# Block-causal attention before two feed-forward layers: split fp32r operands against unsplit fp32 on parts of the TensorE array

## The chip, the cores and the metric

The kernel runs on one core of a Trainium2 chip. The metric is the device time of one execution in microseconds (us). TensorE (PE) multiplies, VectorE (DVE), ScalarE (ACT) and GpSimd (POOL) do the rest, and one queue (SP) issues every DMA. The working memory is SBUF; TensorE writes to PSUM, which has eight banks of 512 fp32 columns on 128 partitions.

## The reference

```python
def _attn_ref(q, k, v):                 # 4 batches, 8 heads, 576 positions, 64 channels
    scores = np.matmul(q, k.transpose(0, 1, 3, 2)) / np.sqrt(64)
    mask = pos[:, None] // 64 >= pos[None, :] // 64      # causal by blocks of 64
    scores = np.where(mask, scores, -1e9)
    attn = np.exp(scores - scores.max(-1, keepdims=True))
    attn = attn / (attn.sum(-1, keepdims=True) + 1e-09)
    return np.matmul(attn, v)

x = attn_out with its heads side by side                  # 2304 tokens x 512
h = x @ w_in;  x = (h * sigmoid(h)) @ w_out               # 512 -> 2048 -> 512
h = x @ w2_in; x = (h * sigmoid(1.702 * h)) @ w2_out
```

## The kernel before

The 32 heads are worked in 16 pairs: head A of a pair lies on partitions 0 to 63, head B on 64 to 127. Queries and keys come with the channels on partitions, 576 positions in the free direction, in nine bands (`j`) of 64 queries. Band `j` needs keys 0 to 64 (j + 1), so its scores have 64 to 576 columns.

TensorE multiplies in fp32r, a form of which one pass over the array keeps only part of the fp32 digits. So every operand is split into a high half (a copy rounded to fp32r) and a low half (the rest), and each product is three: high by high, high by low, low by high. For the scores (`s_mm`, lines 452 to 454) the queries of both heads are laid out block-diagonally in a tile `bd`, so that one 128 x 128 weight tile makes a band of 64 queries of both heads. `q_hi`, `q_lo`, `k_hi` and `k_lo` make the halves, `q_put` lays the query halves into `bd` by DMA. `s_max` takes the row maxima from PSUM on VectorE, `s_exp` the exponential and the row sums on ScalarE. `t_mm` (line 517) transposes the probabilities by TensorE, four 128 x 128 blocks to a bank, 25 blocks a pair. `t_hi` copies a bank out as the high half, `t_lo` (line 535) subtracts for the low half. `o_mm` (line 554) multiplies by the values, whose halves `v_hi` and `v_lo` make: the weights are high and low values side by side, 64 columns each, and the high and low probabilities stream past them. So the result has the part of the high values on the upper 64 partitions and that of the low values on the lower ones, for each head, in two ranges of bands (`halves`). `o_copy` takes these out of PSUM, `x_shift` moves three halves by DMA between partitions, `x_add` adds them on GpSimd and `x_norm` (line 587) multiplies by the reciprocals of the row sums. The reciprocals go through `r_add`, `r_inv`, a transpose (`r_mm`), `r_copy`, a write to DRAM (`r_put`) and a read that spreads them over 64 partitions (`r_get`).

The result `xy` has 512 channels on four groups of 128 partitions and 2304 tokens. The feed-forward layers (`phase`, `evac`) take up to 512 tokens at a time: per 128 hidden channels 12 products up (lines 697 to 699), tanh, and 12 down (lines 724 to 726). The weights come as fp64 and are turned into fp32 and split on VectorE, ScalarE and GpSimd (`w_scale` to `w_split`, lines 265 to 306), two pieces per 128 hidden channels.

The order of instructions is worked out at build time. Each piece of work is an `Op` with an engine, an expected duration, what it reads and writes, and an urgency. `Flow.run` goes through expected time and always gives an engine its most urgent piece that is ready. For attention the urgency is in `plan`, one number for each step of a pair, and `TAU` from pair to pair; attention goes ahead of the feed-forward layers (`BEFORE`). `EARLY` holds back single weight pieces. The engines then work in that order, each waiting for what it needs. At the start `NWARM` products on zeros run until the first scores.

SBUF is shared in time. Attention's tiles lie in pools `a1` to `a6`; a pool that attention has finished with is closed, and a pool of the feed-forward layers (`l1` to `l6`) opens in its place. `HOME` says which pool a feed-forward tile lies in, so the first weight tiles wait for the first pools of attention to close.

Of the kernel before, what the change touches and what calls it, by code (L numbers as in the profile page):

```python
# [22 lines left out]
class Op:  # L23
    __slots__ = ("eng", "us", "fn", "at", "lag", "size", "left", "outs", "ready", "end", "name", "idx", "sb")


class Flow:
# [3 lines left out]
    SEM = 0.06  # L31
    LAG = {"pe": 0.2, "act": 0.1, "dve": 0.08, "pool": 0.04, "sp": 0.0, "none": 0.0}
# [6 lines left out]
    def add(self, eng, us, fn, reads=(), writes=(), at=0.0, lag=0.0, size=0, after=(), name="", sb=False, early=0.0):  # L39
        op = Op()  # L40
        op.eng, op.us, op.fn, op.at, op.lag, op.size, op.name = eng, us, fn, at, lag, size, name
        op.outs, op.ready, op.end, op.idx, op.sb = [], early, 0.0, len(self.ops), sb
# [35 lines left out]
    def run(self, log=None):  # L78
# [3 lines left out]
        dma = 0.0  # L82
        now = {}
# [7 lines left out]
        while n < len(self.ops):  # L91
# [11 lines left out]
            us = op.us  # L103
            other = "pool" if op.sb else "dve" if e == "pool" and self.dve_sb else None
# [24 lines left out]
def act(n):  # L129
    return 0.06 + n * 0.833e-3  # L130
# [14 lines left out]
def block_causal_attention_two_ffn(  # L145
# [25 lines left out]
    NS = 10  # L171
    NWF = 8
    EARLY = [40.4, 125.4, 119.6, 162.9, 164.5, 84.4, 75.8, 216.7, 81.4, 12.3, 74.1, 229.3]
# [3 lines left out]
    NWARM = 12  # L177
    TAU = 12.6
# [11 lines left out]
    stacks = {x: ExitStack() for x in ("a1", "a2", "a3", "a4", "a5", "a6")}  # L190
    pools = {"cst": open_pool(ctx, "cst"), "psum": open_pool(ctx, "psum", space=PSUM)}
    pools["drp"] = open_pool(ctx, "drp", space=bass.MemoryType.DRAM)
    for x in ("a6", "a5", "a4", "a3", "a2"):
        pools[x] = open_pool(stacks[x], x, side="right")
    pools["a1"] = open_pool(stacks["a1"], "a1")
# [9 lines left out]
    bank = {i: T("psum", [P, 512], F32, f"bank{i}") for i in (0, 1, 4, 5, 6, 7)}  # L205
    sb = T("psum", [P, 2, 512], F32, "sb")
    bank[2], bank[3] = sb[:, 0, :], sb[:, 1, :]
    YB, HB = (2, 3, 6, 7), (0, 1, 4, 5)
# [3 lines left out]
    one = T("cst", [P, 1], F32, "one")  # L212
    yd = [T("drp", [P, ND, NT], F32, f"yd{i}") for i in range(2)]

    def xkeys(m, c0, n):
# [6 lines left out]
    HOME = {"xc0": 1, "ws0_0": 1, "th0": 1, "ws0_1": 2, "g0": 2, "ws1_0": 2, "th1": 2, "ws1_1": 3, "g1": 3, "ws2_0": 3,  # L222
            "ws2_1": 4, "ws3_0": 4, "ws3_1": 4, "g2": 4, "g3": 4, "yst0": 4, "yst1": 4, "ws4_0": 5, "ws4_1": 5, "ws5_0": 5,
            "yst2": 5}

    def home(x):
        return f"l{HOME.get(x, 6)}"
# [5 lines left out]
    def slot_after(n, i):  # L233
        return [opened[home(f"ws{n % NS}_{i}")]]

# [75 lines left out]
    flat = [(kt, j) for kt in range(NKT) for j in range(2 * kt, NB)]  # L311
    fidx = {x: i for i, x in enumerate(flat)}
    nat = len(flat)
    groups = [list(range(i, min(i + 4, 21))) for i in range(0, 21, 4)] + [list(range(21, 25))]
    q0 = NB // 2
    halves = [(0, q0), (q0, NB)]

# [4 lines left out]
    def op(eng, us, fn, reads=(), writes=(), lag=0.0, size=0, sb=False):  # L322
        x = add(eng, us, fn, reads, writes, clock[0] - BEFORE, lag=lag, size=size, name=tag[0], sb=sb)
        for k in [*reads, *writes]:
            odd = len(k) > 1 and k[1] == 1
            if k[0] in ("q", "k", "qh", "ql"):
                where = "a1"
            elif k[0] in ("bd", "kh", "kl"):
                where = "a2" if odd else "a1"
            elif k[0] == "pj":  # L330
                where = "a5" if odd else "a3"
            else:
                where = "a4" if k[0] == "pt" and not odd else "a6"
            ends[where].append(x)
        return x

    def bd(p, i):
        return T("a2" if p % 2 else "a1", [P, NB, P], F32R, f"bd{p % 2}{i}")

    def kbd(p, i):  # L340
        return [("bd", p % 2, i, r) for r in range(2)]

    def pj(p, j):
        return T("a5" if p % 2 else "a3", [P, P * (j // 2 + 1)], F32, f"p{p % 2}_{j}")
# [4 lines left out]
    def a1(p, n):  # L349
        two = n in ("kh", "kl")  # L350
        return T("a2" if two and p % 2 else "a1", [P, S], F32 if n in "qk" else F32R, n + (str(p % 2) if two else ""))

    def ka1(p, n):
        return (n, p % 2 if n in ("kh", "kl") else 0)

    def a3(p, n, shape=None, dt=F32):
        return T("a6", shape or [P, S], dt, f"{n}_{p % 2}")

    def pt(p, i):
        return T("a6" if p % 2 else "a4", [P, nat, P], F32R, f"pt{i}_{p % 2}")  # L360

    def copy(eng, o, i):
        if eng == "act":
            return lambda: nc.scalar.copy(o, i)  # L364
        if eng == "pool":
            return lambda: nc.gpsimd.tensor_mul(o, i, one.to_broadcast(list(i.shape)))
        return lambda: nc.vector.tensor_copy(o, i)

    US = {"act": act, "dve": dve, "pool": pool}
    turn = {"t": 0, "o": 0}  # L370
    ring = {"t": (4, 5), "o": (6, 7)}
    S_BANK = (0, 1, 1, 2, 3, 1, 0, 1, 2)
    held = {}

    def take(what, key):
        if what == "s":
            held[key] = S_BANK[key[2]]
        else:
            turn[what] += 1
            held[key] = ring[what][turn[what] % len(ring[what])]  # L380
        return held[key]

    def src(p, n):
        if p == 0 and n in "qk":
            return a3(0, {"q": "e0", "k": "e1"}[n]), ("e", 0, "qk".index(n))
# [448 lines left out]
```

## Time and profile before

| | |
|---|---|
| median of 3 runs | 997.97 us (997.46 to 1000.44) |
| profiled execution, first to last instruction | 996.9 us |
| the same execution, outside that span | not recorded; the median is 1.1 us above the span |
| PE busy | 977.5 us, 98% of the span |
| DVE busy | 689.1 us, 69% |
| ACT busy | 479.9 us, 48% |
| POOL busy | 296.6 us, 30% |
| granted TensorE clock, mean | 0.998 of 2.4 GHz |

Busy time is the time in which at least one instruction of an engine is under way. TensorE's instructions overlap: the next product starts while the one before is still leaving the array. So a full PE row says that it always had something under way, and not that each column came as fast as it can. The distance between two starts tells more than a duration.

### The profile page before, as it was taken

How to read it: one execution, taken by the hardware profiler on the slowest of the kernel's cores; microseconds unless marked ns; L12 is line 12 of the kernel's file. 1: busy time of each engine (PE TensorE's matmuls, PEld its weight loads, DVE VectorE, ACT ScalarE, POOL GpSimd, SP SyncE). 2: the span in 40 equal slices, each digit the busy share in tenths (PEclk: the TensorE clock that was granted, in tenths of full speed). 3: DMA queues.
4: the chain of work that ended last, by engine and by line, in shares of the span. 5: the costliest groups of instructions: out<-in, count | busy, mean ns of one | idle time of the engine just before them, and what ended most of it. 6: DMA issues, size and time to landing. Idle time of an engine off the chain costs nothing.

```text
span 996.9 us, 14425 instructions
## 1 busy us (share of the span) xinstructions
PE 977.5 (98%) x5196; PEld 841.5 (84%) x5196; DVE 689.1 (69%) x1151; ACT 479.9 (48%) x1055; POOL 296.6 (30%) x231
## 2 busy tenths in 40 slices
PE   7999999999999999999999999999999999999998
PEld 6899989878888888898888898888898888988887
DVE  6888888999898977379873479953378444544433
ACT  6888878845555543254333254432354332333221
POOL 7587767840213332044310054210053000000000
PEclk9999999999999999999999999999999999999999
DMA  7887887532354434323420112420112222112222
GB/s 182 201 195 193 223 198 194 131 106 106 127 187 152 137 123 162 108 85 127 144 87 23 43 43 74 138 105 1 43 64 85 85 85 85 64 64 85 85 85 85
DMA packets 84473, 112.38 MB, mean 113 GB/s; under 512 B 41904, under 2 KB 46512, under 8 KB 84400
## 3 DMA queue, kind: packets, MB, share of 16 engines
q1 hardware_dynamic: 84400, 111.45, 36.9%
q8 instruction: 41, 0.67, 0.3%
q14 instruction: 32, 0.26, 0.1%
HBM read 71.83 MB, written 23.67 MB: 96 GB/s over the span
## 4 chain that ended last, share of the span: by engine, by line
PE 88%; DVE 5%; ACT 2%; POOL 2%; DMA 1%; issue 1%; SPq 0%; DVEq 0%; POOLq 0%; ACTq 0%
PE bank L698 13%; PE bank L699 13%; PE bank L697 13%; PE sb L726 7%; PE sb L724 7%; PE sb L725 6%; PE bank L726 6%; PE bank L725 6%; PE bank L724 6%; PE bank L517 3%; PE bank L554 3%; DVE mx L465 2%; DVE pt L535 1%; ACT p L475 1%; PE bank L452 1%
## 5 line engine op out<-in xcount | busy, mean ns | idle before, releaser
L714 DVE SCALAR_TENSOR_TENSOR th<-th,bank 128x512 f32<-128x512 f32 (+1 forms) x160 | 100.8, 630 | 197.6 <-ACT th L712 197.3
L697 PE MATMUL bank<-xc,ws 128*128 128x512 f32 (+1 forms) x640 | 236.1, 369 | 0.0
L698 PE MATMUL bank<-xc,ws 128*128 128x512 f32 (+1 forms) x640 | 235.6, 368 | 0.0
L699 PE MATMUL bank<-xc,ws 128*128 128x512 f32 (+1 forms) x640 | 235.5, 368 | 0.0
L712 ACT ACTIVATE th<-bank 128x512 f32<-128x512 f32 (+1 forms) x160 | 88.7, 555 | 297.9 <-PE bank L699 295.6
L717 DVE TENSOR_TENSOR g<-th,g 128x512 fp32r<-128x512 f32 (+1 forms) x160 | 126.7, 794 | 40.2 <-ACT g L716 38.7
L716 ACT CAST g<-th 128x512 fp32r<-128x512 f32 (+1 forms) x160 | 92.5, 579 | 110.0 <-DVE th L714 109.8
L306 POOL TENSOR_TENSOR ws<-wf,ws 128x512 fp32r<-128x512 f32 x50 | 71.7, 1443 | 228.1 <-ACT ws L304 226.8
L697 PEld LDWEIGHTS bank<-xc,ws 128*128 128x128 f32 x640 | 120.7, 189 | 20.2
L698 PEld LDWEIGHTS bank<-xc,ws 128*128 128x128 f32 x640 | 120.7, 189 | 19.9
L699 PEld LDWEIGHTS bank<-xc,ws 128*128 128x128 f32 x640 | 120.6, 188 | 20.0
L297 POOL TENSOR_TENSOR wf<-wf,wt 128x512 f32<-128x512 f32 x52 | 75.7, 1456 | 193.8 <-DVE wt L288 192.5
L726 PE MATMUL sb<-g,ws 128*128 128x512 f32 (+1 forms) x320 | 118.0, 369 | 1.5 <-DVE g L717 1.5
L724 PE MATMUL sb<-g,ws 128*128 128x512 f32 (+1 forms) x320 | 118.1, 369 | 0.1
L724 PE MATMUL bank<-g,ws 128*128 128x512 f32 (+1 forms) x320 | 117.8, 368 | 0.0
L725 PE MATMUL sb<-g,ws 128*128 128x512 f32 (+1 forms) x320 | 117.8, 368 | 0.0
L726 PE MATMUL bank<-g,ws 128*128 128x512 f32 (+1 forms) x320 | 117.7, 368 | 0.0
L725 PE MATMUL bank<-g,ws 128*128 128x512 f32 (+1 forms) x320 | 117.7, 368 | 0.0
L678 DVE TENSOR_TENSOR xc<-xy,xc 128x512 fp32r<-128x512 f32 (+1 forms) x117 | 78.2, 688 | 15.3 <-PE bank L698 8.5
L673 ACT CAST xc<-xy 128x512 fp32r<-128x512 f32 (+1 forms) x120 | 66.9, 575 | 20.8 <-PE bank L698 19.6
L535 DVE TENSOR_TENSOR pt<-bank,pt 128x512 fp32r<-128x512 f32 (+1 forms) x112 | 68.5, 625 | 8.2 <-ACT pt L364 8.0
L726 PEld LDWEIGHTS sb<-g,ws 128*128 128x128 f32 x320 | 60.3, 188 | 11.9 <-DVE g L717 1.9
(79 smaller groups left out, 1611.8 us busy)
## 6 DMA issues: line engine op xcount, KB each, us to landing
raw<-w SPq DMA_DIRECT2D x64, 512.0 KB, 3.2
yd<-yst SPq DMA_DIRECT2D x64, 256.0 KB, 2.3
yst<-yd SPq DMA_DIRECT2D x64, 256.0 KB, 3.5
v<-vP SPq DMA_DIRECT2D x16, 320.0 KB, 4.7
rb<-rd SPq DMA_DIRECT2D x32, 144.0 KB, 3.0
x<-e SPq DMA_DIRECT2D x32, 144.0 KB, 2.4
q<-qT SPq DMA_DIRECT2D x15, 288.0 KB, 4.4
k<-kT SPq DMA_DIRECT2D x15, 288.0 KB, 4.6
```

The costliest lines, as they stand in the source:

```text
L535: op("dve", dve(n), lambda: nc.vector.tensor_sub(lo, bank[b][:, :n], f32(hi)), [("B", b), ("pt", p % 2, g, 0)], [("pt", p % 2, g, 1)])
L678: add(lo[0], lo[1], lambda view=view, s=s, lo=lo: lo[2].tensor_sub(view(1), s, f32(view(0))), xkeys(kt, c0, n) + [Kh], [Kl], tx, after=[op ...
L697: nc.tensor.matmul(h, w[:, 0, c], view(0), start=kt == 0, stop=False)
L698: nc.tensor.matmul(h, w[:, 1, c], view(0), start=False, stop=False)
L699: nc.tensor.matmul(h, w[:, 0, c], view(1), start=False, stop=kt == ND - 1)
L712: add("act", act(n), lambda th=th, h=h: nc.scalar.activation(th(), h, AF.Tanh, scale=0.5 if l == 0 else 0.851), [("B", b)], [kth], t, afte ...
L714: add("dve", dve(n), lambda th=th, h=h: nc.vector.scalar_tensor_tensor(out=th(), in0=th(), scalar=1.0, in1=h, op0=ALU.add, op1=ALU.mult), ...
L716: add("act", act(n) + 0.05, lambda th=th, g=g: nc.scalar.copy(g(0), th()), [kth], [kgh], t, after=e2)
L717: add("dve", dve(n) + 0.01, lambda th=th, g=g: nc.vector.tensor_sub(g(1), th(), f32(g(0))), [kth, kgh], [kgl], t, after=e2, sb=True)
L724: nc.tensor.matmul(y, w[:, 0, c], g(0), start=st, stop=False)
L725: nc.tensor.matmul(y, w[:, 1, c], g(0), start=False, stop=False)
L726: nc.tensor.matmul(y, w[:, 0, c], g(1), start=False, stop=sp)
```

## The change

Attention is written anew on fp32 operands as they come; the feed-forward layers keep their arithmetic.

- No halves are made: `q_hi`, `q_lo`, `q_put`, `k_hi`, `k_lo`, `v_hi`, `v_lo`, `t_lo` go, with the block-diagonal tiles. `q_scale` multiplies the queries by 1/8 in place on GpSimd. Queries and keys have three buffers, values two.
- Scores: each product takes 64 channels of one head (64 rows of the array) and 64 queries (64 columns). Head A of an even band uses the quarter from the upper rows to the upper output partitions and head B that from the lower to the lower; for an odd band they are crossed. An even and an odd band stand next to each other in `ROUNDS`, so four products in a row use four quarters. Three groups (`PARTS`) make up a pair. The widest band takes banks 0 and 1; bands share banks 2 to 4.
- Probabilities leave PSUM by one copy per bank (`t_cp`), laid out so that a value product reads bands two apart by a step.
- Values: one head makes the upper 64 output partitions and the other the lower ones, on 64 columns of the array each; even bands in one group, odd bands (heads crossed) in another, both through bank 7.
- `x_out` multiplies from PSUM by the reciprocals straight into `xy` on VectorE; `o_copy`, `x_shift`, `x_add`, `x_norm` go. `r_put` writes the reciprocals in three parts, because the heads of odd bands are crossed.
- The tokens of `xy` stand in the order even bands (8, 6, 4, 2, 0), then odd bands (1, 3, 5, 7). The host puts the output rows back in order.
- The pools: the first feed-forward tiles (four weight slots of two tiles, and others) lie in `l1`, which is open from the start; the rest waits for the pools `a2` and `a3`. The banks of the feed-forward stage are numbered anew. Plan, `TAU`, `EARLY` and `NWARM` (3, now on fp32) are new, and the planner counts a change of the array's division as 0.1 us.

The core of the diff (removed functions are printed above, and the new plan is left out):

```diff
-    NWARM = 12
-    TAU = 12.6
+    NWARM = 3
+    TAU = 49.027
...
+    def q_scale(p):
+        q, k = src(p, "q")
+        op("pool", 1.15, lambda: nc.gpsimd.tensor_mul(q, q, scale.to_broadcast([P, S])), [k, "scale"], [k])
+
+    PARTS = [[(8, 0, 0), (7, 2, 0)], [(6, 3, 0), (0, 3, 448), (5, 4, 0)], [(4, 2, 0), (2, 2, 320), (3, 3, 0), (1, 3, 320)]]
+    ROUNDS = [
+        [(8, 0, 512, 0), (7, 0, 512, 0), (8, 512, 64, 512), (7, 0, 64, 0)],
+        [(6, 0, 448, 0), (5, 0, 448, 0), (0, 0, 64, 0), (5, 0, 64, 448)],
+        [(4, 0, 320, 0), (3, 0, 320, 0), (2, 0, 192, 0), (1, 0, 192, 0)],
+    ]
...
-                nc.tensor.matmul(o, bd(p, 0)[:, j, :], kh[:, c], start=True, stop=False)
-                nc.tensor.matmul(o, bd(p, 0)[:, j, :], kl[:, c], start=False, stop=False)
-                nc.tensor.matmul(o, bd(p, 1)[:, j, :], kh[:, c], start=False, stop=True)
+            for j, c, n, o in ROUNDS[part]:
+                for h, r in enumerate((A, B)):
+                    t = s_out(j)[B if (h + j) % 2 else A, o:o + n]
+                    nc.tensor.matmul(t, q[r, j * BLK:(j + 1) * BLK], k[r, c:c + n], start=True, stop=True)
...
+        for h in range(2):
+            op("sp", 0.4, lambda h=h: nc.sync.dma_start(out=rd[ne:, 1 - h], in_=rt[ne:, h]), [("rt", p % 2)],
+               [("rd", p % 2, 1 + h)])
...
+    def t_cp(p, g, eng):
+        b = held["t", p, g]
+        n = len(ROWS[g]) * P
+        o = pt(p)[:, 4 * g:4 * g + len(ROWS[g]), :].rearrange("p a b -> p (a b)")
+        op(eng, US[eng](n) + 0.08, copy(eng, o, bank[b][:, :n]), [("B", b)], [("pt", p % 2, g)])
...
+        js = ODDS if odd else EVENS
+        seq = [(kt, [j for j in js if j >= 2 * kt]) for kt in range(NKT)]
...
+            for a, (kt, x) in enumerate(seq):
+                f = PLACE[x[0], kt]
+                c = js.index(x[0]) * BLK
+                for h, r in enumerate((A, B)):
+                    hh = (1 - h if odd else h) * BLK
+                    y = pt(p)[:, f:f + 4 * len(x) - 3:4, hh:hh + BLK]
+                    nc.tensor.matmul(bank[b][r, c:c + len(x) * BLK], v[:, (2 * kt + h) * BLK:(2 * kt + h + 1) * BLK], y,
+                                     start=a == 0, stop=a == len(seq) - 1)
...
+    def x_out(p, odd):
+        b, hp = divmod(p, PPB)
+        c, n = o_cols(odd)
+        rb = buf(p, "rb", [P, S])
+        op("dve", dve(n) + 0.1, lambda: nc.vector.tensor_mul(xy[:, hp, b * S + c:b * S + c + n], bank[OB[odd]][:, :n], rb[:, c:c + n]),
+           [("B", OB[odd]), ("rb", p % 2, 0), ("rb", p % 2, 1)], xkeys(hp, b * S + c, n))
```

## Rows read from the trace of the kernel before

**Rows 1.** The page, busy time and the span in 40 slices

```profile
PE 977.5 (98%) x5196; PEld 841.5 (84%) x5196; DVE 689.1 (69%) x1151; ACT 479.9 (48%) x1055; POOL 296.6 (30%) x231
...
PEclk9999999999999999999999999999999999999999
```

**Rows 2.** Busy time by stretches: stretch, length, busy of each engine, clock, DMA

```profile
60.00:100.00 40.00, 39.46 (x295) 37.07 (x296) 34.21 (x73) 33.60 (x102) 33.49 (x28) 1.00 0.80 197
...
200.00:220.00 20.00, 17.73 (x89) 14.40 (x88) 18.77 (x26) 7.93 (x17) 10.77 (x7) 1.00 0.36 104
...
400.00:600.00 200.00, 200.00 (x1007) 170.73 (x1006) 131.13 (x193) 79.62 (x148) 49.41 (x34) 1.00 0.24 82
```

**Rows 3.** Instructions in order of time: start, duration, engine, line

```profile
117.66 0.28 PE L453 MATMUL bank<-kl,bd 128*128 128x64 f32 x1
...
117.77 0.28 PE L454 MATMUL bank<-kh,bd 128*128 128x64 f32 x1
...
118.66 0.60 PE L517 MATMUL bank<-ident,p 128*128 128x128 f32 x4
...
162.39 1.89 PE L554 MATMUL bank<-pt,va 128*128 128x320 f32 x14
164.21 0.28 PE L489 MATMUL bank<-ident,r 128*9 128x128 f32 x1
...
219.66 0.39 PE L697 MATMUL bank<-xc,ws 128*128 128x512 f32 x1
...
231.44 0.39 PE L698 MATMUL bank<-xc,ws 128*128 128x512 f32 x1
```

**Rows 4.** TensorE in order of time: the start, and the widest band

```profile
7.68 0.39 PE L453 MATMUL sb<-kl,bd 128*128 128x256 f32 x1 [1.56 <-POOL kl L419]
...
9.30 0.40 PE L452 MATMUL sb<-kh,bd 128*128 128x288 f32 x1 [0.17 <-ACT p L475]
...
180.25 0.38 PE L452 MATMUL sb<-kh,bd 128*128 128x288 f32 x1
```

**Rows 5.** Waits from 20 to 180 us: total, times, longest

```profile
PEld bank L517 <- DVE pt L535: 6.5, 11, 1.8
...
PEld bank L452 <- ACT p L475: 3.4, 7, 0.9
```

**Rows 6.** Groups by form, 0 to 240 us: busy us, mean ns, idle before

```profile
L535 DVE TENSOR_TENSOR pt<-bank,pt 128x512 fp32r<-128x512 f32 x96 | 64.5, 683 | 8.2 <-ACT pt L364 8.0
L517 PE MATMUL bank<-ident,p 128*128 128x128 f32 x400 | 63.5, 281 | 6.3 <-DVE pt L535 5.3 <-ACT p L475 0.5 <-ACT rt L495 0.4
...
L366 POOL TENSOR_TENSOR kh<-k,one 128x576 fp32r<-128x576 f32 x15 | 17.7, 1182 | 9.8 <-PE bank L454 9.7
L400 DVE SCALAR_TENSOR_TENSOR ql<-q,qh 128x576 fp32r<-128x576 f32 x15 | 16.7, 1116 | 3.7 <-ACT qh L397 3.3 <-DMA v<-vP 0.4
...
L475 ACT ACTIVATE p<-sb,mx 128x576 f32<-128x576 f32 x16 | 12.1, 756 | 1.2 <-DVE mx L465 1.2
L465 DVE TENSOR_REDUCE mx<-sb 128x1 f32<-128x576 f32 x16 | 11.9, 747 | 1.7 <-PE sb L454 1.0 <-ACT p L475 0.7
...
L276 DVE SCALAR_TENSOR_TENSOR wf<-wf,wt 128x512 int32<-128x512 int32 x9 | 7.8, 880 | 0.0
...
L274 DVE TENSOR_SCALAR wt<-wf 128x512 int32<-128x512 int32 x9 | 3.7, 413 | 0.0
```

**Rows 7.** The chain that ended last: 170 to 250 us by line, then the start

```profile
by line: PE bank L697 9.2%; PE bank L699 9.1%; PE bank L698 9.1%; DMA rb<-rd 8.2%; issue 7.2%; POOL x L582 5.8%; POOL va L430 4.2%; POOL xy L587 4.1%; POOL ws L306 3.3%; PE sb L726 3.2%; POOL xc L678 3.2%; POOL va L366 3.1%; PE sb L724 2.9%
...
0.73 2.78 DMA e<-qT
```

**Rows 8.** DMA issues: size each, median us from issue to landing

```profile
rb<-rd SPq DMA_DIRECT2D x32, 144.0 KB, 3.0
```

**Rows 9.** One stretch by engine, and TensorE inside it

```profile
140.00:145.00 5.00, 3.95 (x19) 3.72 (x20) 4.22 (x8) 1.89 (x4) 4.92 (x5) 0.66 0.65 154
...
141.05 1.97 PE L517 MATMUL bank<-ident,p 128*128 128x128 f32 x8 [1.58 <-DVE pt L535]
```

More of the change, by code (lines that the diff above doesn't have):

```diff
@@ L82, in run @@
         dma = 0.0
+        mode = 0
         now = {}
@@ L320, in block_causal_attention_two_ffn, with op, buf @@
     tag = ["att"]
-    def op(eng, us, fn, reads=(), writes=(), lag=0.0, size=0, sb=False):
-        x = add(eng, us, fn, reads, writes, clock[0] - BEFORE, lag=lag, size=size, name=tag[0], sb=sb)
+    def op(eng, us, fn, reads=(), writes=(), lag=0.0, size=0, sb=False, mode=0):
+        x = add(eng, us, fn, reads, writes, clock[0] - BEFORE, lag=lag, size=size, name=tag[0], sb=sb, mode=mode)
         for k in [*reads, *writes]:
[L325 to L334, printed above, removed]
-        return x
[L337 to L341, printed above, removed]
+            ends["a2" if k[0] in ("q", "k", "pj") else "a3"].append(x)
+        return x
+    def buf(p, n, shape, pool="a3", dt=F32):
+        return T(pool, shape, dt, f"{n}_{p % 2}")
     def pj(p, j):
-        return T("a5" if p % 2 else "a3", [P, P * (j // 2 + 1)], F32, f"p{p % 2}_{j}")
+        return buf(p, f"p{j}", [P, P * (j // 2 + 1)], "a2")
     def kpj(p, j):
         return ("pj", p % 2, j)
[L349 to L360, printed above, removed]
     def copy(eng, o, i):
@@ L497, in rd_, with rt_, r_copy @@
+    def rt_(p):
+        return buf(p, "rt", [NB, P])
+    def r_copy(p, eng):
+        b = held["r", p]
+        op(eng, 0.2, copy(eng, rt_(p), bank[b][:NB, :P]), [("B", b)], [("rt", p % 2)])
     def rd_(p):
@@ L511, in t_mm, with pt @@
+    ROWS = [[(8, i) for i in range(4)], [(6, i) for i in range(4)], [(4, 0), (4, 1), (4, 2), (1, 0)],
+            [(2, 0), (2, 1), (3, 1), (3, 0)], [(0, 0), (5, 2), (5, 1), (5, 0)], [(7, i) for i in (3, 2, 1, 0)], [(8, 4)]]
+    PLACE = {x: 4 * r + i for r, row in enumerate(ROWS) for i, x in enumerate(row)}
+    def pt(p):
+        return buf(p, "pt", [P, len(PLACE), P])
     def t_mm(p, g):
-        b = take("t", ("t", p, g))
+        b = t_bank(("t", p, g))
         def mms():
-            for i, f in enumerate(groups[g]):
-                kt, j = flat[f]
+            for i, (j, kt) in enumerate(ROWS[g]):
@@ L559, in e_ @@
-    def e_(p, h):
-        return a3(p, f"e{h}")
-    def ke(p, h):
-        return ("e", p % 2, h)
-    def o_copy(p, h, half, eng):
-        j0, j1 = halves[half]
-        n = (j1 - j0) * BLK
-        b = held["o", p, h, half]
-        keys = [(*ke(p, h), half)] + ([ke(p, h)] if p == 0 else [])
-        op(eng, US[eng](n), copy(eng, e_(p, h)[:, j0 * BLK:j1 * BLK], bank[b][:, :n]), [("B", b)], keys)
-    def x_shift(p, i):
-        x = a3(p, "x")
-        dst, h, r = [(x[A], 0, B), (x[B], 1, A), (e_(p, 0)[B], 1, B)][i]
-        ks = [(*ke(p, h), z) for z in range(2)]
-        kd = [[("x", p % 2, 0)], [("x", p % 2, 1)], [(*ke(p, 0), z) for z in range(2)]][i]
-        op("sp", 0.65, lambda: nc.sync.dma_start(out=dst, in_=e_(p, h)[r]), ks, kd, size=P * S * 2)
@@ L638, in attention @@
         for p in range(NP):
             for i, (when, fn, *args) in enumerate(plan):
[L640 to L644 removed]
+                if p > 0 or (fn, args) not in ((load, ["q"]), (load, ["k"])):
+                    clock[0], tag[0] = p * TAU + when, f"{p}.{i}"
+                    fn(p, *args)
@@ L646, in swap @@
+        for k in range(2, 4):
             def swap(k=k):
@@ L832 @@
     r = run_bass_kernel_spmd(nc, [arrays], core_ids=[0])
-    return np.ascontiguousarray(r.results[0]["out"].T)
+    y = r.results[0]["out"].T.reshape(B, S // D, D, H * D)
+    order = [*range(S // D - 1, -1, -2), *range(1, S // D, 2)]
+    return np.ascontiguousarray(y[:, np.argsort(order)].reshape(B * S, H * D))
```

308 lines of the change are left out of this document (105 added, 203 removed).

## The prediction

> **What bounds the kernel now.** I read the page first, then busy time by stretches, then the groups by form for the first 240 us, and last TensorE's instructions in order of time. The page puts PE at 98% of the span and the granted clock at nine tenths or more in all 40 slices [rows 1]. An average says little here, because the program has two stages: attention until about 209 us, and two feed-forward layers after it. By stretches PE is full in the second stage (200.00 of 200 us) and nearly full in the first (39.46 of 40), where VectorE has 34.21 and ScalarE 33.60 [rows 2]. The feed-forward part keeps its work and cannot start in earnest before attention is done, so what attention gains or loses moves the end one for one, as long as the weights are ready.
>
> A busy PE hides how much of it is latency, so I price its work by the distance between starts. Back-to-back products start 0.2265 us apart at 512 columns (the two rows from 219.66 to 231.44 us stand 52 products apart) and 0.11 apart at 64; four transposes last 0.60 us [rows 3] where one lasts 0.28 [rows 6], so each adds 0.107; fourteen value products take 1.82 us up to the next start [rows 3]. One pair of heads before is then: scores in ten pieces of three products each; by columns 0.11 three times (64, 128, 192), 0.12 (256), 0.13 twice (288), 0.145, 0.175, 0.205 and 0.2265 (320, 384, 448, 512), the ones between drawn in a line between the two ends, together 1.46, times three 4.4 us. Values are two times fourteen products, 3.6. Transposes are 25 and one for the reciprocals, 26 x 0.107 = 2.8. Sum 10.8 us. The widest band of scores (two pieces of 288 columns) starts at 9.30 us for pair 0 and at 180.25 for pair 15, the last of 16 [rows 4]: 170.95 / 15 = 11.40 us a pair. So PE's own work is 95% of the period and 0.6 us is holes, which the waits put on transposes waiting for VectorE to empty a bank and on scores waiting for the exponential that frees theirs [rows 5].
>
> **The change on TensorE.** Three products become one on unsplit operands, and products of 64 columns of output share the array: four at a time for scores, two for values. No row of before multiplies unsplit fp32 (the transposes only pass data). From below, such a product costs one pass, 0.2265 us at 512 columns. From above I take four passes: the split form makes three partial products of the halves and leaves out low by low, and an exact product has all four; 4 x 0.2265 / 512 = 1.77 ns a column, an estimate from those rows. I take the upper value. Along one quarter the columns of a pair are 512 + 64, 448 + 64 and 320 + 192 = 1600, so scores cost 2.83 us if the four quarters run together. For the values, bands of even number have 320 + 256 + 192 + 128 + 64 columns and odd ones 256 + 192 + 128 + 64, again 1600 and 2.83 us if the halves run together. Transposes stay at 2.8. Sum 8.44 us against 10.8. With only two of the four quarters together scores would be 5.7, and values without overlap 5.7.
>
> Each group of scores (three a pair) or values (two) also changes how the array is divided, up to ten changes a pair. A lone transpose lasts 0.28 us where one in a row adds 0.107; if each change empties the array it costs that difference, 0.17, so the term lies between 0 and 1.7 us a pair. I take half, 0.85, since some groups stand next to each other. The Trainium skill, "TensorEngine Tiling (Array Packing)", section Tiling Modes, says that changing the tiling mode drains the engine. By it the term is the full 1.7 and my time 14 us later. No run shown here has a change of mode.
>
> Of the 0.6 us of holes I keep half, for the reason in the next part. Period: 8.44 + 0.85 + 0.3 = 9.59 us. Gain: 16 x (11.40 - 9.59) = 29.0 us.
>
> **The change on the other engines.** VectorE's 34.21 of 40 us are 9.75 a pair. It loses six low halves of the probabilities of 0.683 and a small one, the low query half of 1.116 [rows 6], a cast and a copy: about 6.2. It gains four plain copies of 512 columns, taken at the same 0.683, a small one, and two normalizing products over 576 columns together, 0.9: about 4.0. That leaves 7.6. Conversion of weights may move into this stage: one piece is two pairs of instructions like those of 0.413 and 0.880 [rows 6], 2.6 us, and eight pieces over 16 pairs are 1.3. VectorE is then at up to 8.9, just under PE's 9.3 (8.44 + 0.85) and not far under it. ScalarE only loses: the casts of both halves, the query half, three copies, for two copies. GpSimd is busy 33.49 of 40 us [rows 2], some 9.5 a pair, nearly all of it splitting keys and values, adding the heads' halves and normalizing; that goes for one product of 576 columns, 1.18 [rows 6]. GpSimd's work is a quarter of the chain between 170 and 250 us [rows 7], so its going may give up to 3 us there (PE is idle 2.27 of 200 to 220 us [rows 2]); on the other hand pair 15 now ends with a three-part write of its reciprocals in place of one. I book 0, bounds 3 us either way.
>
> Seven transfers of about 144 KB a pair go and two small ones come, on the one issuing queue. In the output path the bank of the values now waits for the reciprocals that are written out and read back (3.0 us to landing for the read alone [rows 8]), then for the normalizing product, and the second group of value products wants the same bank. Behind a waiting value product on PE stands everything else. Two buffers of reciprocals and the written order cover it if value products are placed a pair later; uncovered, read and product are some 4 us a pair, more than the gain.
>
> Score banks: the widest ring is scores 8 and 7 (1.0 us and 0.2 latency), two maxima (0.747 for the wider), two exponentials (0.756) [rows 6], in all 4.2; then scores 4 and 2 through one of the same banks, smaller, about 2.9; with six hand-overs of 0.1 some 7.7. It fits into 9.6 only while little queues in it.
>
> Start: the warm-up is twelve single passes before and three products of four passes after, the same. Then the first scores wait for the low half of the keys until 7.68 [rows 4]. The new path needs one scaling of 1.18 after a load that lands at 3.51 [rows 7], so it is ready before the warm-up ends near 5.8. I book 1.9 us.
>
> Sum: 29.0 + 1.9 = 30.9. The profiled span is 996.9 and the median of the runs 997.97, so about 1.1 us lies around the span, and stays. 997.97 - 30.9 = 967.1, forecast **967 us**.
>
> **Rivals.** (1) VectorE or the ring of score banks binds. For it: 8.9 and 7.7 above. If four steps of the ring each stand behind one instruction of 0.7 us, it takes 10.5; gain 16 x 0.9 + 1.9 = 16.3, hence 982. Against: the same engines had more to do in before, and PE still ran at 95%.
>
> (2) Changes of mode cost next to nothing and the holes close: 8.9 a pair, 16 x 2.5 + 1.9 = 42, hence 956; with the 3 us at the transition and none of either, 8.44 a pair, 946.
>
> (3) The other side: the quarters do not run together. Both heads of a band write one PSUM bank, the array's upper rows to one half of its partitions and the lower rows to the other. If these take turns, scores cost 5.7 and the period is 12.42: 16 x 1.02 - 1.9 = 14 slower, hence 1012. It decides from the point where some 1.9 of the 2.83 us saved by this overlap are lost. Before never runs two products side by side, so no row speaks for or against. The Trainium skill, same page, section Restrictions and Gotchas, says that different row tiles cannot access one PSUM bank at the same time. By that rule this rival would be the forecast. I give it a small chance of its own, as the two heads touch different partitions of the bank.
>
> (4) The clock falls. Between 140 and 145 us, with PE busy only 3.95 of 5, the granted clock was 0.66, and eight transposes lasted 1.97 us where 0.28 + 7 x 0.107 is 1.0 [rows 9]: part of that stretch ran at 1.2 GHz instead of 2.4. If holes grow and 30% of the attention work runs at the lower level, a pair costs 2.5 more, 12.1, and 16 x 0.7 - 1.9 = 9 slower, hence 1007. From about 23% on it eats the gain. Against: nine tenths or more in every slice of the page.
>
> (5) The saving is real and goes into waits at the value bank, the period stays near 11.4: within 0.3%.
>
> **How the numbers follow.** Forecast 0.45 (own range 958 to 976), rival 1 0.20, rival 2 0.12, rival 3 0.12, rival 4 0.06, rival 5 0.05. A measurement of this kernel tells about 0.3%, 3 us, from no change. Faster is 0.45 + 0.20 + 0.12 = 0.77, same 0.05, slower 0.18. The range leaves out the far end of rival 2, most of rival 3 and half of rival 4, some 0.17 together: 951 to 1005.
>
> **What would show it.** Right: score products of four quarters starting almost together, a 512-column one holding its quarter about 0.9 us; the widest band returning every 9.6 us; GpSimd nearly empty before 200 us; feed-forward products at full rate near 180 us instead of 209; PE still the largest share of the chain. Wrong: score products of a pair one after the other (rival 3), a granted clock well under 1.00 in several stretches of attention (rival 4), PE waiting mostly for maxima, copies or the reciprocals (rivals 1 and 5), or an unsplit product that costs other than four passes, which moves 5.7 of the 8.44 us.

## The result and the profile after

The changed kernel takes 964.51 us (median of 4 runs, 964.40 to 964.92) against 998.26 of before on the same chip (4 runs, 997.46 to 1000.44): a ratio of 0.9654, 95% interval 0.9640 to 0.9668 (the two medians alone give 0.9662). The forecast was 967 us with 951 to 1005.

The page of the changed kernel, the lines that answer to [rows 1], the slices of GpSimd, and the chain:

```profile
PE 951.1 (99%) x5606; PEld 775.5 (81%) x5606; DVE 644.7 (67%) x1102; ACT 424.7 (44%) x925; POOL 174.0 (18%) x144
...
POOL 2211101211223321452200263200061000000000
...
PE 97%; DVE 2%; ACT 1%; issue 0%; POOL 0%; DVEq 0%; ACTq 0%; POOLq 0%
```

PE makes 97% of the chain that ended last, and GpSimd, a quarter of it at the end of attention in [rows 7] (2% of the whole chain of before), is off it. Busy time by stretches (as [rows 2]):

```profile
0.00:20.00 20.00, 15.28 (x120) 8.17 (x124) 10.11 (x31) 9.23 (x30) 5.56 (x12) 0.91 0.44 152
60.00:100.00 40.00, 40.00 (x458) 27.30 (x460) 32.21 (x72) 26.06 (x90) 5.80 (x9) 1.00 0.44 138
100.00:140.00 40.00, 40.00 (x464) 27.20 (x459) 32.88 (x75) 25.28 (x85) 5.56 (x8) 1.00 0.43 134
```

From 60 to 140 us PE has no hole at all, VectorE is busy four fifths, GpSimd 5.80 of 40 us where it had 33.49. TensorE in order of time (start, duration, line; 393 scores, 430 and 472 transposes, 500 values): the widest band of pairs 0 and 1, then one whole period:

```profile
6.80 0.60 PE L393 MATMUL s<-k,q 64*64 64x512 f32 x2
...
16.66 0.65 PE L393 MATMUL s<-k,q 64*64 64x512 f32 x2
...
139.93 0.65 PE L393 MATMUL s<-k,q 64*64 64x512 f32 x2
139.94 0.65 PE L393 MATMUL bank<-k,q 64*64 64x512 f32 x2
140.41 0.59 PE L393 MATMUL s<-k,q 64*64 64x512 f32 x2
140.42 0.60 PE L393 MATMUL bank<-k,q 64*64 64x512 f32 x2
140.84 0.22 PE L393 MATMUL s<-k,q 64*64 64x64 f32 x2
...
141.06 0.28 PE L430 MATMUL bank<-ident,r 128*9 128x128 f32 x1
...
141.38 1.31 PE L500 MATMUL bank<-pt,v 128*64 128x256 f32 x16
142.62 1.09 PE L472 MATMUL bank<-ident,p 128*128 128x128 f32 x8
143.64 1.09 PE L393 MATMUL bank<-k,q 64*64 64x320 f32 x16
144.66 1.85 PE L500 MATMUL bank<-pt,v 128*64 128x320 f32 x20
146.44 1.10 PE L472 MATMUL bank<-ident,p 128*128 128x128 f32 x8
147.47 1.10 PE L393 MATMUL bank<-k,q 64*64 64x448 f32 x16
148.50 1.09 PE L472 MATMUL bank<-ident,p 128*128 128x128 f32 x8
149.52 0.65 PE L393 MATMUL s<-k,q 64*64 64x512 f32 x2
```

Read the starts. The two widest bands, both heads of each (`x2`), start 0.01 us apart: four quarters at once. An unsplit product stands there as two records (both heads make `x2` of each); the second half starts 0.48 us after the first (139.93, 140.41) and gives way 0.43 after that (140.84), so a 512-column product holds its quarter 0.91 us. The whole period is 149.52 - 139.93 = 9.59 us, without an idle time in brackets anywhere. Pair 0 starts its widest band at 6.80 (9.30 before), pair 15 at 149.52 (180.25 before, [rows 4]). That is 142.72 / 15 = 9.51 us on average: eleven of the fifteen periods are 9.59, one is 9.74, and the first three are 9.86, 8.43 and 9.17.

That splits the 34.1 us between the spans (996.9 to 962.8). The start gives 9.30 - 6.80 = 2.5. Fifteen periods give 170.95 - 142.72 = 28.2. What follows the widest band of pair 15 gives the rest, 816.65 - 813.28 = 3.4.

### The profile page after: what moved, and what is told of

It is laid out like the page before. It is cut to its first block, busy times and chain, and to the rows that moved or that the text cites. A ratio compares the mean times of both kernels' runs of the same rounds, so it can differ in the third digit from the quotient of the medians.

```text
span 962.8 us, 14863 instructions
## 1 busy us (share of the span) xinstructions
PE 951.1 (99%) x5606; PEld 775.5 (81%) x5606; DVE 644.7 (67%) x1102; ACT 424.7 (44%) x925; POOL 174.0 (18%) x144
## 4 chain that ended last, share of the span: by engine, by line
PE 97%; DVE 2%; ACT 1%; issue 0%; POOL 0%; DVEq 0%; ACTq 0%; POOLq 0%
PE bank L625 13%; PE bank L626 13%; PE bank L624 13%; PE s L597 7%; PE s L598 7%; PE s L599 7%; PE bank L597 7%; PE bank L598 7%; PE bank L599 7%; PE bank L472 5%; PE bank L500 5%; PE bank L393 3%; PE s L393 1%; PE bank L532 0%; ACT p L411 0%
## 5 line engine op out<-in xcount | busy, mean ns | idle before, releaser
L625 PE MATMUL bank<-g,ws 128*128 128x512 f32 (+1 forms) x640 | 235.5, 368 | 0.0
L624 PE MATMUL bank<-g,ws 128*128 128x512 f32 (+1 forms) x640 | 235.4, 368 | 0.0
L626 PE MATMUL bank<-g,ws 128*128 128x512 f32 (+1 forms) x640 | 235.4, 368 | 0.0
L617 DVE TENSOR_TENSOR g<-th,g 128x512 fp32r<-128x512 f32 (+1 forms) x160 | 128.6, 806 | 40.6 <-ACT g L616 38.8
L624 PEld LDWEIGHTS bank<-g,ws 128*128 128x128 f32 x640 | 120.7, 189 | 20.1
L625 PEld LDWEIGHTS bank<-g,ws 128*128 128x128 f32 x640 | 120.7, 189 | 19.9
L626 PEld LDWEIGHTS bank<-g,ws 128*128 128x128 f32 x640 | 120.7, 189 | 19.8
L597 PE MATMUL s<-xc,ws 128*128 128x512 f32 (+1 forms) x320 | 118.9, 372 | 2.5 <-ACT th L612 1.2
L614 DVE SCALAR_TENSOR_TENSOR th<-th,bank 128x512 f32<-128x512 f32 (+1 forms) x80 | 50.4, 630 | 103.2 <-ACT th L612 103.2
L614 DVE SCALAR_TENSOR_TENSOR th<-th,s 128x512 f32<-128x512 f32 (+1 forms) x80 | 50.5, 631 | 102.5 <-ACT th L612 97.7
L598 PE MATMUL s<-xc,ws 128*128 128x512 f32 (+1 forms) x320 | 117.9, 368 | 0.0
L597 PE MATMUL bank<-xc,ws 128*128 128x512 f32 (+1 forms) x320 | 117.9, 368 | 0.0
L598 PE MATMUL bank<-xc,ws 128*128 128x512 f32 (+1 forms) x320 | 117.8, 368 | 0.0
L599 PE MATMUL s<-xc,ws 128*128 128x512 f32 (+1 forms) x320 | 117.8, 368 | 0.0
L599 PE MATMUL bank<-xc,ws 128*128 128x512 f32 (+1 forms) x320 | 117.7, 368 | 0.0
L612 ACT ACTIVATE th<-bank 128x512 f32<-128x512 f32 (+1 forms) x80 | 44.5, 556 | 156.8 <-PE bank L599 151.1
L612 ACT ACTIVATE th<-s 128x512 f32<-128x512 f32 (+1 forms) x80 | 44.5, 556 | 147.5 <-PE s L599 143.6
```

The source lines that it names most:

```text
L597: nc.tensor.matmul(h, w[:, 0, c], view(0), start=kt == 0, stop=False)
L598: nc.tensor.matmul(h, w[:, 1, c], view(0), start=False, stop=False)
L599: nc.tensor.matmul(h, w[:, 0, c], view(1), start=False, stop=kt == ND - 1)
L612: add("act", act(n), lambda th=th, h=h: nc.scalar.activation(th(), h, AF.Tanh, scale=0.5 if l == 0 else 0.851), [("B", b)], [kth], t, afte ...
L614: add("dve", dve(n), lambda th=th, h=h: nc.vector.scalar_tensor_tensor(out=th(), in0=th(), scalar=1.0, in1=h, op0=ALU.add, op1=ALU.mult), ...
L617: add("dve", dve(n) + 0.01, lambda th=th, g=g: nc.vector.tensor_sub(g(1), th(), f32(g(0))), [kth, kgh], [kgl], t, after=e2, sb=True)
```

## The experiments

All times are medians; ratios are to the kernel before, run on the same chip. Differences to the changed kernel are taken from its 964.51 us; the runs come from several chips, on which the kernel before took 998.26 to 999.09 us.

**Score bands in turn.** The main term of the sum rests on four quarters at once, so the bands of a group were put one after the other.

```diff
-        [(8, 0, 512, 0), (7, 0, 512, 0), (8, 512, 64, 512), (7, 0, 64, 0)],
-        [(6, 0, 448, 0), (5, 0, 448, 0), (0, 0, 64, 0), (5, 0, 64, 448)],
-        [(4, 0, 320, 0), (3, 0, 320, 0), (2, 0, 192, 0), (1, 0, 192, 0)],
+        [(8, 0, 512, 0), (8, 512, 64, 512), (7, 0, 512, 0)],
+        [(6, 0, 448, 0), (0, 0, 64, 0), (5, 0, 384, 0)],
+        [(4, 0, 320, 0), (2, 0, 192, 0), (3, 0, 256, 0), (1, 0, 128, 0)],
```

> The changed kernel (964.5 us) with the score bands of a group one after the other instead of an even and an odd one side by side; both heads of a band still stand next to each other, and the filler columns are gone. All other instructions and their order stay. Theory (TensorE's own work sets the period, four quarters run together): the columns along one quarter go from 1600 to 2880 a pair, 1280 more at 1.77 ns, 2.3 us a pair, 36 us in all: 1001 us. Rival (the heads of a band take turns at their bank, so that only two quarters ever work together): the order of the bands changes nothing, 962 to 967 us. Rival (another engine sets the period and TensorE has room): well under half of the 36.

Measured: 964.03 us, ratio 0.9647 (0.9634 to 0.9660). Next to nothing changed: 0.5 us. By the expectation that speaks for the rival, but the trace shows something else (TensorE in order of time, this run):

```profile
91.82 0.65 PE L393 MATMUL s<-k,q 64*64 64x512 f32 x2
91.85 0.65 PE L393 MATMUL bank<-k,q 64*64 64x512 f32 x2
92.30 0.60 PE L393 MATMUL s<-k,q 64*64 64x512 f32 x2
92.33 0.59 PE L393 MATMUL bank<-k,q 64*64 64x512 f32 x2
92.73 0.28 PE L393 MATMUL s<-k,q 64*64 64x64 f32 x4
92.94 0.28 PE L430 MATMUL bank<-ident,r 128*9 128x128 f32 x1
```

Band 7 (`bank`) is behind both products of band 8 (`s`) in the program, yet it starts 0.03 us after the first and 0.88 before the second. Each quarter took the next product meant for it, so the edit did not take the overlap away. The period is 9.55 us in this run, against 9.59. The group lasts 92.94 - 91.82 = 1.12 us for 576 + 512 columns. If only two quarters could work together it would last 1088 columns at 0.91 us per 512, 1.9 us. So the rival falls by the length of the group, not by the time of the run. A version that puts both bands on the same two quarters was not run.

**Heads in turn in the value products.**

```diff
-            for a, (kt, x) in enumerate(seq):
-                ...
-                for h, r in enumerate((A, B)):
+            for h, r in enumerate((A, B)):
+                for a, (kt, x) in enumerate(seq):
+                    ...
```

> The changed kernel with the value products of head A of a group all ahead of those of head B, instead of alternating. Theory (two column halves run together, TensorE sets the period): 1600 columns a pair more at 1.77 ns, 2.8 us, 45 us in all: 1010 us, less a little where the last product of one head stands beside the first of the other. Rival (the halves do not overlap as it is): 962 to 967 us. Rival (another engine sets the period): well under half of the 45.

Measured: 999.03 us, ratio 1.0000 (0.9991 to 1.0009): 34.5 us slower than the changed kernel, the whole gain. TensorE in order of time, the even group, the odd one, and what follows the odd one:

```profile
88.76 3.19 PE L500 MATMUL bank<-pt,v 128*64 128x320 f32 x20
91.89 1.09 PE L472 MATMUL bank<-ident,p 128*128 128x128 f32 x8
...
96.41 2.12 PE L500 MATMUL bank<-pt,v 128*64 128x256 f32 x16
98.46 1.09 PE L472 MATMUL bank<-ident,p 128*128 128x128 f32 x8
```

The even group takes 3.13 us where it took 146.44 - 144.66 = 1.78, the odd one 2.05 where it took 1.24: 2.16 a pair, times 16 34.6 us, the measured difference. The halves do run together in the changed kernel, and TensorE's time comes through to the end of the run unreduced. It is short of the forecast 45: columns are cheaper than 1.77 ns (below), and the ends of the two heads overlap by some 0.26 us a group. The overlap can be seen in the single records of the even group, where each head has five products of two records: the second head starts at 90.12, behind seven records of the first and ahead of its last three (90.22, 90.33 and 90.39). So it slipped past three records, where band 7 had slipped past six of the eight records of band 8. What sets how far a product can slip was not measured.

**A product in the middle of the scores, and the same among the transposes.** These price one change of the array's division.

```diff
-            for j, c, n, o in ROUNDS[part]:
+            for i, (j, c, n, o) in enumerate(ROUNDS[part]):
+                if part == 1 and i == 2:
+                    nc.tensor.matmul(bank[4][:, 448:512], ident, ident[:, :BLK], start=True, stop=True)
```

> The changed kernel with one product more a pair: 128 x 128 weights, 64 columns, unsplit fp32, in the middle of the second group of scores, whose products use quarters of the array; its result is overwritten. It costs its own time and two changes of the array's division. Theory (each change costs 0.13 us, read from the nine changes of a period): 0.2 us for itself and 0.26 for the changes, 16 x 0.46 = 7 us: 972 us, and 4 us more than the same product among the transposes. Rival (changes cost nothing, the 1.15 us over the bare sum is something else): 3 to 4 us more than the changed kernel, the same as among the transposes.

```diff
             for i, (j, kt) in enumerate(ROWS[g]):
+                if g == 0 and i == 2:
+                    nc.tensor.matmul(bank[b][:, 2 * P:2 * P + BLK], ident, ident[:, :BLK], start=True, stop=True)
```

> The changed kernel with the same extra product a pair, but in the middle of a group of four transposes, which use the whole array as it does: no change of the array's division. Both theories: its own time, 4 passes of 64 columns or the load of its weights twice, about 0.2 us a pair, 16 x 0.2 = 3 us: 968 us. It is there to be taken off the run with the product among the scores.

Measured: 973.51 us (0.9742, 0.9728 to 0.9755) among the scores, 967.34 us (0.9679, 0.9666 to 0.9693) among the transposes. The latter is 2.8 us over the changed kernel, 0.18 a pair, close to the 0.2 expected. The difference of the two is 6.2 us, 0.39 a pair, for two changes: 0.19 each by the times. By the traces (first the run among the scores, then that among the transposes):

```profile
95.38 0.98 PE L395 MATMUL bank<-k,q 64*64 64x448 f32 x8
96.29 0.43 PE L392 MATMUL bank<-ident 128*128 128x64 f32 x2
96.66 0.34 PE L395 MATMUL bank<-k,q 64*64 64x64 f32 x8
96.93 1.09 PE L474 MATMUL bank<-ident,p 128*128 128x128 f32 x8
```

```profile
90.12 0.87 PE L474 MATMUL bank<-ident,p 128*128 128x128 f32 x6
90.83 0.33 PE L473 MATMUL bank<-ident 128*128 128x64 f32 x2
91.00 0.39 PE L474 MATMUL bank<-ident,p 128*128 128x128 f32 x2
91.32 1.10 PE L393 MATMUL bank<-k,q 64*64 64x448 f32 x16
```

The score group goes from 148.50 - 147.47 = 1.03 us to 96.93 - 95.38 = 1.55, 0.52 more. Eight transposes go from 1.02 to 1.20, 0.18 more. That leaves 0.34 for two changes, 0.17 each, where 0.13 was expected. The traces are the better source here: the run among the scores also started its first widest band 1.28 us later than the other (8.19 against 6.91), which no change of the array's division makes. So a change costs about 0.17 us between scores and the whole array, and the rival that it costs nothing falls.

**Two and four more instructions on VectorE.**

```diff
+    def v_more(p):
+        w = tiles["warm"]
+        for _ in range(2):
+            op("dve", 0.0, lambda: nc.vector.tensor_mul(w, w, w), ["warm"], ["warm"])
...
-        (754.78, o_mm, 1), ...
+        (600.00, v_more), (754.78, o_mm, 1), ...
```

> The changed kernel with two more instructions of 128 x 512 on VectorE a pair (a tile of zeros squared in place), some 0.62 us each, which nothing waits for; all other instructions and their order stay. Theory (TensorE's work sets the period of 9.6 us; VectorE is busy 32.2 of 40 us, 7.7 a pair, and 9.0 with the two): under 2 us more, 964 to 967 us. Rival (VectorE or the ring of score banks sets the period): 16 x 1.24 = 20 us more, 984 us.

> The same with four more instructions a pair. Theory (TensorE sets the period until VectorE has more to do): 7.7 + 4 x 0.62 = 10.2 us of VectorE a pair against 9.6, so VectorE takes over, 16 x 0.6 = 10 us more, 974 us, and up to 16 us if its copies come late for the transposes. Rival (VectorE or the ring sets it already): 16 x 2.5 = 40 us more, 1004 us. Rival (VectorE's busy share overstates what it must do): under 3 us.

Measured: 987.68 us (0.9885, 0.9871 to 0.9900) with two, 1007.95 us (1.0088, 1.0073 to 1.0103) with four: 23 and 43 us more, near what the rival forecast. But the experiment did not do what it was meant to. VectorE in order of time, the run with two:

```profile
6.29 16.87 DVE L509 TENSOR_TENSOR warm<-warm 128x512 f32<-128x512 f32 x21 [4.17 <-PE bank L537]
23.08 1.81 DVE L403 TENSOR_REDUCE mx<-bank 128x1 f32<-128x448 f32 x4
24.80 0.75 DVE L403 TENSOR_REDUCE mx<-s 128x1 f32<-128x576 f32 x1
25.47 7.95 DVE L509 TENSOR_TENSOR warm<-warm 128x512 f32<-128x512 f32 x11
```

The added work waited only for the tile of zeros, so the planner put all 32 instructions at the start, 21 ahead of the first maxima and 11 right behind them. They hold VectorE for 16.87 + 7.95 = 24.8 us once: the first period takes 31.51 us instead of 9.86, and from the fourth on this run has 9.59 like the changed kernel (one is 9.74 in both). So it says nothing of the steady state. With four a pair, 42 of the 64 stand in the first 40.6 us. The next run ties each to a pair.

**One more instruction on VectorE, in step.**

```diff
+    def v_more(p):
+        w = tiles["warm"]
+        op("dve", 0.0, lambda: nc.vector.tensor_mul(w, w, w), ["warm", ("pt", p % 2, 5)], ["warm"])
```

> The run with two more instructions a pair put all of them into the first 40 us (they waited only for the tile of zeros), so it told nothing of the steady state. Now one more of 128 x 512 a pair, in VectorE's order behind the copy of the fifth group of transposes of each pair, 0.8 us each by that run; nothing waits for its result, and the order of all other instructions stays. Theory (TensorE's own work sets the period; VectorE with 7.7 + 0.8 = 8.5 us a pair stays under 9.6, and its copies have room): under 3 us more, 964 to 967.5 us. Prediction's first rival (VectorE or the ring of score banks sets the period): 16 x 0.8 = 13 us more, 977 us; half of it, 971 us, if they are as tight as TensorE.

Measured: 966.86 us, ratio 0.9677 (0.9664 to 0.9690): 2.4 us more, where the instruction lasts 0.68 us here and sixteen of them 10.9. Busy time by stretches in this run:

```profile
60.00:100.00 40.00, 40.00 (x462) 27.30 (x460) 33.93 (x77) 26.21 (x90) 6.56 (x8) 1.00 0.43 125
100.00:140.00 40.00, 39.35 (x453) 26.80 (x449) 34.46 (x76) 25.64 (x88) 6.26 (x8) 1.00 0.47 142
```

VectorE has more to do and PE stays full in the first stretch, with a small hole in the second. By pairs, eleven of the fifteen periods keep their length within 0.01 us, and four are 0.5 to 0.9 us longer (10.39, 10.10, 10.10 and 10.61). So TensorE sets the period in most pairs, and in four VectorE's order had less room than one such instruction; what sets those four apart was not looked at.

**Value products of the first key block alone.** This leaves out the values of all keys but the first 128, and so takes TensorE work away to see what lies behind it.

```diff
+        use = seq[:1]
...
-            for a, (kt, x) in enumerate(seq):
+            for a, (kt, x) in enumerate(use):
```

> The changed kernel without the value products of all key blocks but the first; the attention output is then that of the first 128 keys. All other instructions stay in their order. It takes TensorE work away and shows what binds next. Columns a pair go from 1600 to 576, 1.8 us less, so 7.8 a pair on TensorE. Theory (TensorE alone sets the period and the next bound lies under 7.8 us): 16 x 1.8 = 29 us less, 936 us. Prediction's first rival (VectorE at up to 8.9 us or the ring of score banks at 7.7 and more stands close behind): only 10 to 20 us less, 945 to 954 us, with TensorE waiting for maxima, exponentials or copies.

Measured: 946.14 us, ratio 0.9472 (0.9456 to 0.9487): 18.4 us less, not 29. Busy time from 60 to 100 us, and two of the waits from 20 to 130 us (total, times, longest):

```profile
60.00:100.00 40.00, 38.05 (x391) 22.81 (x391) 35.33 (x82) 29.37 (x102) 5.79 (x9) 1.00 0.47 143
```

```profile
PEld bank L472 <- DVE pt L344: 9.1, 15, 1.0
...
PEld bank L472 <- ACT p L411: 5.4, 11, 0.5
```

PE now has holes, 1.95 of 40 us, before transposes that wait for VectorE's copies and ScalarE's exponentials. The period is 8.31 to 8.34 us in most pairs, 1.3 under that of the changed kernel, where TensorE's own work, without 1024 columns at 1.68 ns (below), is an estimated 7.87. The prediction's first rival was not what sets the time, but it stands where it was priced, between 7.7 and 8.9.

**No filler columns.** The uneven rounds of the first experiment, in the original order:

```diff
+        [(8, 0, 512, 0), (7, 0, 512, 0), (8, 512, 64, 512)],
+        [(6, 0, 448, 0), (5, 0, 384, 0), (0, 0, 64, 0)],
+        [(4, 0, 320, 0), (3, 0, 256, 0), (2, 0, 192, 0), (1, 0, 128, 0)],
```

> The changed kernel without the score columns that no one reads (64 columns of band 7 computed twice, 64 to 128 columns too many in bands 5, 3 and 1), which stand beside a wider product in another quarter. Theory (the widest of the four quarters sets the time, and the others are free beside it): no change, 963 to 966 us. Rival (columns cost in whatever quarter): about 4 of 45 blocks of columns a head less, up to 5 us faster. Rival (a group with uneven quarters loses its place in step, and the next product waits): some us slower.

Measured: 963.87 us, ratio 0.9648 (0.9634 to 0.9663): 0.6 us less. The intervals of the ratios do not tell that from nothing; in the trace the period is 9.55 us against 9.59, as it was with the bands in turn, which also had no filler, and 16 x 0.04 is 0.6. Columns in a narrower quarter are all but free beside a wider one, and uneven quarters do no harm.

**Eight changes instead of nine.**

```diff
-        ... (552.04, t_mm, 6), ... (340.98, r_mm), ...
+        ... (710.00, t_mm, 6), ... (710.00, r_mm), ...
```

> The changed kernel with other urgencies for the transpose of the reciprocals and for the one-block group of transposes, so that the first value group of a period follows a score group at once and these two transposes go in front of the next eight: eight changes of the array's division a pair instead of nine. Theory (each change costs 0.13 us, whichever it is): 16 x 0.13 = 2 us less, 962.4 us. Rival (a change between two divided arrays costs as much as two through the whole array, or the later reciprocals make the normalizing product late): no gain or slower, 964 to 970 us.

Measured: 971.87 us, ratio 0.9730 (0.9717 to 0.9743): 7.4 us more instead of 2 less. TensorE in order of time:

```profile
96.56 0.33 PE L472 MATMUL bank<-ident,p 128*128 128x128 f32 x1
96.72 0.27 PE L430 MATMUL bank<-ident,r 128*9 128x128 f32 x1
97.27 1.09 PE L472 MATMUL bank<-ident,p 128*128 128x128 f32 x8 [0.28 <-DVE pt L344]
```

The two small transposes each take one of the two banks that the transposes share, directly ahead of eight that need both. TensorE then waits for VectorE's copy; from 96.72 to 97.27 it starts nothing, where 0.12 is usual. That is 0.43 a pair, and the period is 10.00 us (94.19 - 84.19) instead of 9.59. Without the wait it would be 9.56: of the 0.17 us of the change that is saved (the value group follows the scores at once) only 0.03 is seen. Nine of the fifteen periods are longer by 0.4, 3.6 us together. The other 3 us between the two spans (969.4 and 962.8) come behind 124 us, where the value groups stand in another order than in the changed kernel; 1.6 of them are idle time of TensorE between 200 and 300 us (98.40 us busy, against 100.00). Neither forecast had the wait or the other order.

**The table loaded early, and both.**

```diff
+        first = T("cst", [P, 1], F32, "first")
+        op("act", 1.4, lambda: nc.scalar.activation(first, scale, AF.Exp), ["scale"], ["first"])
```

> The changed kernel with one exponential of 128 x 1 on ScalarE at the very start, so that the table it needs is loaded before the first maxima are there. In the changed kernel the load of 1.28 us stands at 7.86 us, after the first maximum and ahead of the first exponential; TensorE then idles 2.94 us, and the granted clock is 0.50 from 12 to 14 us. Theory (the load is on the chain, and the idle time behind it also costs the clock): 1.3 us for the load and up to 2 for twelve transposes that took 3.0 instead of 1.5 us: 961 to 963 us. Rival (the load is hidden later by holes that the start has anyway): 964 to 965 us. Rival (the clock falls anyway): 963.2 us.

> Both edits together, the table loaded early and eight changes a pair. Theory: the gains add, 959 to 961 us. Rival: each is hidden by the other or by waits, 962 to 965 us.

Measured: 962.52 us (962.12 to 963.12), ratio 0.9637 (0.9623 to 0.9650), and 969.30 us (0.9703, 0.9690 to 0.9717) for both. The early table alone is 2.0 us under the changed kernel, as expected; the ranges of the runs do not touch, the intervals of the ratios overlap by 0.001. ScalarE and TensorE at the start, the changed kernel and then this one:

```profile
7.86 1.28 ACT L411 ACT_TABLE_LOAD   x1 [7.86 <-DVE mx L403]
...
10.89 1.28 PE L393 MATMUL bank<-k,q 64*64 64x320 f32 x16 [2.94 <-ACT p L411]
12.10 3.01 PE L472 MATMUL bank<-ident,p 128*128 128x128 f32 x12
```

```profile
0.71 1.28 ACT L536 ACT_TABLE_LOAD   x1 [0.71 <-PEq L727]
...
7.54 0.60 PE L393 MATMUL s<-k,q 64*64 64x512 f32 x2
...
10.44 1.09 PE L393 MATMUL bank<-k,q 64*64 64x320 f32 x16 [1.74 <-ACT p L411]
...
15.15 0.65 PE L393 MATMUL s<-k,q 64*64 64x512 f32 x2
```

TensorE's idle time shrinks from 2.94 to 1.74 us, by the load. That is 1.2 of the 2.0 us. From the widest band of pair 0 to that of pair 1 the changed kernel takes 16.66 - 6.80 = 9.86 us and this run 15.15 - 7.54 = 7.61. The traces of the heads in turn and of the eight changes, with the late load but a full clock there, take 8.80. So the load accounts for 1.2 us, and the fallen clock of the changed kernel's profiled run (0.50 from 12 to 14 us, while twelve transposes take 12.10 to 15.04) for about 1.1. Against that, this run's first scores happened to start 0.74 us later; with unchanged code for the start, the widest band of pair 0 stands between 6.80 and 8.19 us in the traces. Of the changed kernel's four runs two had a mean clock of 0.998 and two of 1.000, at 964.56 and 964.92 against 964.47 and 964.40; only the first of the four was profiled, so whether a later start hides the clock in the others stays open. This is the fastest version that was run with all of the work in it.

## Why the prediction was right, step by step

The forecast was 967, the result 964.5. The mechanism is the one forecast: TensorE sets the period before and after, and its own work became shorter. The product among the transposes and the heads in turn both show that a microsecond of TensorE is a microsecond of the run; sixteen VectorE instructions in step show up with a fifth of their length, all of it in four periods.

The period was forecast at 9.59 us and the steady one measured at 9.59. That the two agree to the digit is luck, since three terms that make it up were off and cancel:

- Columns: 1.77 ns forecast. From the second half of a 512-column product to the next start in its quarter 0.43 us pass, twice that for both halves, 0.86 / 512 = 1.68 ns. Two times 1600 columns cost 5.38 us, not 5.66. That is 3.8 passes at the pace of the split products (0.2265 us for 512 columns), so the four passes taken from the split form were nearly right; why one costs a little less here was not tested.
- Changes of division: 0.85 forecast, as half of ten at 0.17. The period above has nine, and they cost what the columns and the transposes (26 x 0.107 = 2.78 us) leave of it: 9.59 - 5.38 - 2.78 = 1.43 us, 0.16 each, close to the 0.17 of the two extra products. The upper bound was nearly right and the halving wrong. The Trainium skill, "TensorEngine Tiling (Array Packing)", section Tiling Modes, says that changing the tiling mode drains the engine, and the 0.16 to 0.17 us agree with it.
- Holes: 0.3 forecast, none found from 60 to 140 us.

So the three errors are -0.28, +0.58 and -0.30 us.

The mean period fell by 28.2 / 15 = 1.88 us. TensorE's own work, 10.8 by the prediction's sum and 9.59 now, is 1.2 of that; most of the rest is holes of before that closed, of which the prediction kept half. They were not spread evenly, as a mean suggests: the four periods of before from 130.28 to 180.25 us, with the stall of [rows 9] in them, take 12.49 us on average. Which engine's relief closed them, no run takes apart.

The gain between the spans is 34.1 us, against 30.9 forecast. Fifteen periods gave 28.2 against 27.2. The start gave 2.5 against 1.9, in a profiled run with an early start and about 1.1 us lost to the clock right after. Behind the widest band of pair 15 came 3.4, against 1.8 for the last period and 0 booked for the transition; the bound there was 3 either way, and the gain fits GpSimd leaving the chain, which no run here tested by itself. (Of the quarter that the prediction read from [rows 7], 6.5% is work of the feed-forward layers, lines 306 and 678, which stays.) The price at the start was the table load at 7.86 us, which the prediction did not see: before, ScalarE's first work was the scaling of queries, which waited for a DMA anyway and had the table loaded meanwhile.

The rivals. The first (VectorE or the bank ring) does not decide, but the run without most value products puts it 1.3 us behind. The second had its holes right and its changes wrong. The third does not hold: both heads of a band write one bank, and with two bands side by side the group of the widest lasts 1.1 us. The rule of the Trainium skill behind it (same page, section Restrictions and Gotchas) is thus not seen at work here, where two row tiles write different partitions of one bank. The fourth touched only the first 20 us, with about 1.1 us. The fifth does not hold, since the value group waits for its reciprocals nowhere in the period shown.

## What to carry to other kernels

Price a busy engine by the distance between starts, before and after, and by its own work per period; then ask of each edit only what it takes from that engine. Ask whether an unsplit product can share the array before splitting operands to save passes: here three full-array passes lost to some four passes on parts of it, and with the value halves one after the other the whole gain was gone. When an engine's early work is removed, look for what it did on the side, such as loading a table, and when transposes are regrouped, count their banks first. Take a steady period from the list of periods and not from their mean, and the worth of an edit at the start from the distance between two fixed points of the traces.

## What the hardware showed that was not expected

In these runs the parts of the array did not keep the order of the program. Band 7 began 0.03 us after the first product of band 8 and ahead of the second, which stood in front of it; so the order of bands within a group did not matter (964.03 against 964.51 us). With the five products of one head in front, the other head's value products slipped past only the last three of its ten records (3.13 against 1.78 us for the group). Whether the number of products in front, or quarters against halves, makes the difference stays open.

An unsplit fp32 product stands in the trace as two records, at 512 columns 0.43 us apart from start to start once the quarter is running.
